# Attention + MLP + mixer kernel: the key sums enter the scores as a float32r matmul, the causal mask is a constant, and layer-1 weights are converted ahead on another timetable

## The chip, the cores and the metric

One core of a Trainium2 chip runs the whole program in one launch. The metric is the device time of that core in microseconds; three runs of the kernel before are shown, and one more execution was profiled.

## What is computed

Attention over 4 batches and 8 heads (576 tokens, head size 64), then two feed-forward layers of 512 x 2048 x 512; the second is preceded by a rank-32 mixing along the tokens. The first layer norms its input.

```python
s_pos = np.maximum(s, 0.0)
cum = np.cumsum(s_pos, axis=-1)
bias = -(cum[:, :, :, None] - cum[:, :, None, :])
scores = np.where(causal, -1000000000.0, scale * q @ k.T + np.minimum(bias, 0.0))
attn = softmax(scores)                      # + 1e-9 in the denominator
x = attn @ v                                # then, per layer:
ch = np.maximum(xn @ w_ch1, 0.0) @ w_ch2    # layer 0: xn = layernorm(x); x = x + ch
xt = x.transpose(0, 2, 1)
h = xt @ U @ V                              # layer 1: u = x + h^T; out = u + ffn(u)
```

Below the diagonal the bias is a difference of key sums, and a softmax row does not change by a constant, so the kernel only needs, for each head, one number per key: the running sum at the key, minus the sum at the end of the row's block of 128 queries. These "key sums" are made once, in `setup`.

## The kernel before, in words

**Tiling.** Every batch is cut into block A (tokens 0 to 255) and block B (256 to 575). Heads are taken in pairs, the two heads of a pair on partitions 0 to 63 and 64 to 127. A pair is worked in ticks: A has one tick (0, 1), B has the ticks (2), (3) and (4), each a block of 128 queries (64 in tick 4). For each tick there is a `score` (matmuls, a DVE reduction that adds the bias and keeps the row's minimum, Exp on ACT, the division), a `trans` (transposes on PE, eviction into `pT`), and after a pair's last tick a `pv` per head. Operands that need more than float32r are split into a high and a low float32r part (`split`: ACT or DVE makes the high part, DVE or POOL the low one). A0 and A1, the A blocks of batches 0 and 1, go in full float32.

**Bias and mask before.** `setup` writes the key sums to a DRAM tensor `cum_dr`. `bias` (L621) reads them back for every head and tick, copied onto all 128 partitions of a tile `t` (L638; L635 for tick 4, 64 partitions a head), and POOL then writes the mask into each such tile (L642). For the first four heads an identity matmul in float32 (L629) and a copy stand in for the load. The DVE reduction in `score` (L696, L678) adds `t` to the scores in PSUM and writes the result over `t`.

**The layers.** 256 steps, 128 a layer: each step is one block of tokens against one slice `m` of 128 hidden units (16 slices, two halves of eight). A step has 12 matmuls in L1053 to L1055 and 12 in L1087 to L1089. The order of steps is in `GROUPS`: layer 0 takes A0 with A1, A2 with A3, then B0 to B3 alone; layer 1 takes (A0, B0) and so on. Weights arrive as float64 in two words; converting one 512 KB half (`f64_to_f32`, then `split`) costs two passes and a split on DVE and ACT each, and the result is written to a DRAM tensor `w_dr`, from which later steps reload it (L506), eight slices being resident (`WSLOTS`). The first eight slices of layer 0 are converted at the start; the others "ahead" of their use by `w_ahead` (L519: one load of 512 KB, L485 or L487, the conversion, and one write of 512 KB, L526).

**What sets the order.** All operations go to a planner (`Plan`) with a priority, a duration per engine it may run on, and buffers; it writes out a fixed order per engine. All transfers are issued by SP in that order. Positions in steps are given by hand: attention of B2 lies in steps 67 to 86 and of B3 in 76 to 100 (`AT`), the conversions of layer 0's second half in 4 to about 12 (`W0`), those of layer 1's 32 halves evenly in 67 to 128 (`W1`). A gated transfer is not issued before the step at its position. Transfers take `nbytes / 400` ns in the planner's own estimate. Until the first step, spare PE time is filled with matmuls on a tile of ones (L1189).

**Buffers.** `t` has 6 tiles, `pA` and `pB` 2 each (`pT` of A and of B), `qk` 2, `wr` (raw weights) 4, `w` 16 halves, PSUM `ps` 6 and `acc` 2.

Of the kernel before, what the change touches and what calls it, by code (L numbers as in the profile page):

```python
# [85 lines left out]
class Plan:  # L86
# [22 lines left out]
    def op(self, prio, alts, reads=(), writes=(), nbytes=0, gate=None, soft=0.0, hold=(), port=False):  # L109
# [3 lines left out]
        o.prio, o.alts, o.nbytes, o.gate = prio, alts, nbytes, gate  # L113
# [29 lines left out]
    def plan(self, prio, price):  # L143
# [37 lines left out]
        while avail:  # L181
# [35 lines left out]
            if o.nbytes:  # L217
                o.end = dma_free = max(dma_free, s + 1100) + o.nbytes / 400.0
# [92 lines left out]
def mha_ffn_mixer_ffn(ctx: ExitStack, tc, qkv_p, qkv_a, qkv_b, s, g, w1, w2, U, V, out):  # L311
# [10 lines left out]
    sb("attn", dict(qk=2, v=1, pA=2, pB=2, t=6, mx=6, sm=4, rc=4))  # L322
# [27 lines left out]
    def load(prio, nbytes, fn, reads, writes, gate=None):  # L350
        P.op(prio, {"sp": (475, fn)}, reads, writes, nbytes, gate)
# [30 lines left out]
    cum_dr = P.fixed(dr_p.tile([B * H, sum(KEYS)], F32, name="cum_dr"))  # L382
# [5 lines left out]
    cums = []  # L388

    def setup():  # L390
        s_sb, cum = (P.buf("pB", [128, 2, 1344]) for _ in range(2))
        cums.append(s_sb)

        def rel(c0, c1):
            return s_sb.tile.rearrange("p a c -> p (a c)")[:R, c0:c1]

        load(PRO, R * S * 4, lambda: nc.sync.dma_start(s_sb[:R, 0, :S], s), [], [s_sb])
# [4 lines left out]
        dve(PRO, S, lambda: nc.vector.tensor_scalar(out=s_sb[:R, 0, :S], in0=s_sb[:R, 0, :S], scalar1=0.0, scalar2=8.0, op0=ALU.max, op1=ALU.mult),  # L402
            [s_sb], [s_sb], 0.521)
        dve(PRO, S, lambda: nc.vector.tensor_tensor_scan(cum[:R, 0, :S], s_sb[:R, 0, :S], s_sb[:R, 0, :S], 0.0, ALU.add, ALU.max),
            [s_sb], [cum], 1.042)

        for i in range(5):
            dve(PRO, KEYS[i], lambda i=i: nc.vector.tensor_scalar(
                out=rel(COL[i], COL[i] + KEYS[i]), in0=cum[:R, 0, :KEYS[i]], scalar1=cum[:R, 0, KEYS[i] - 1:KEYS[i]], scalar2=None, op0=ALU.subtract),
                [cum] + [s_sb] * (i == 0), [s_sb] if i == 0 else [(s_sb, i)], 0.521, 128)  # L410
        for c, (i0, i1) in enumerate(((0, 2), (2, 5))):
            c0, c1 = COL[i0], COL[i1 - 1] + KEYS[i1 - 1]
            load(PRO + 1 + c, R * (c1 - c0) * 4, lambda c0=c0, c1=c1: nc.sync.dma_start(cum_dr[:, c0:c1], rel(c0, c1)),
                 [(s_sb, i) for i in range(i0, i1)], [(cum_dr, i) for i in range(i0, i1)])
# [117 lines left out]
    class Pair:  # L532
# [11 lines left out]
        def load(self, prio, gate):  # L544
# [76 lines left out]
        def bias(self, prio, tick, gate):  # L621
            idx = self.b * H + 2 * self.p
            ts = self.t[tick] = [P.buf("t", [128, S]) for _ in range(1 if tick[0] == 4 else 2)]
            n = sum(KEYS[i] for i in tick)
            c0 = COL[tick[0]]
            for z, t in enumerate(ts):
                if self.full and idx < 4:
                    c = psum()
                    pe(prio, 4 * mm_cost(384), lambda c=c, z=z: nc.tensor.matmul(  # L629
                        c[:, :n], ident[:R, idx + z:idx + z + 1].to_broadcast([R, 128]), cums[0].tile.rearrange("p a c -> p (a c)")[:R, :n],  # L630
                        start=True, stop=True), [ident, (cums[0], 0), (cums[0], 1)], [c])
                    copy(prio, n, lambda c=c, t=t: t[:, :n], lambda c=c: c[:, :n], [c], [t], psum=True)
                elif tick[0] == 4:
                    for y in range(2):
                        load(prio, 256 * n, lambda t=t, y=y: nc.sync.dma_start(  # L635
                            t[64 * y:64 * (y + 1), :n], cum_dr[idx + y:idx + y + 1, c0:c0 + n].to_broadcast([64, n])), [(cum_dr, 4)], [(t, "y%d" % y)], gate)
# [4 lines left out]
                def mask(t, d, cols, base=0):  # L641
                    return lambda: nc.gpsimd.affine_select(out=d(), in_=d(), compare_op=ALU.is_ge, fill=-8e9, base=base, pattern=cols, channel_multiplier=1)  # L642

                if self.blk == "A":
                    d = lambda t=t: t[:, :512].rearrange("p (a c) -> p a c", c=256)[:, :, :128]
                    P.op(prio, {"pool": (360, mask(t, d, [[0, 2], [-1, 128]]))}, [t], [t])
                elif tick[0] < 4:
# [592 lines left out]
```

## Time and profile before

| | |
|---|---|
| median of 3 runs | 1127.78 us (1126.51 to 1134.36) |
| span of the profiled execution | 1120.7 us |
| PE (matmul) busy | 1076.8 us, 96% |
| PE weight load busy | 1020.9 us, 91% |
| DVE / ACT / POOL busy | 603.9 / 490.3 / 176.1 us |
| data moved | 233.38 MB, mean 208 GB/s |

The median of the runs is 7.1 us above the profiled span. "PE" is the matmul, "PEld" the loading of its stationary operand, which overlaps with it; a matmul's end is modelled, so matmuls that follow each other closely overlap in the rows. The DMA share is the mean busy share of the 16 DMA engines.

### The profile page before, as it was taken

How to read it: one execution, taken by the hardware profiler on the slowest of the kernel's cores; microseconds unless marked ns; L12 is line 12 of the kernel's file. 1: busy time of each engine (PE TensorE's matmuls, PEld its weight loads, DVE VectorE, ACT ScalarE, POOL GpSimd, SP SyncE). 2: the span in 40 equal slices, each digit the busy share in tenths (PEclk: the TensorE clock that was granted, in tenths of full speed). 3: DMA queues.
4: the chain of work that ended last, by engine and by line, in shares of the span. 5: the costliest groups of instructions: out<-in, count | busy, mean ns of one | idle time of the engine just before them, and what ended most of it. 6: DMA issues, size and time to landing. Idle time of an engine off the chain costs nothing.

```text
span 1120.7 us, 21017 instructions
## 1 busy us (share of the span) xinstructions
PE 1076.8 (96%) x7830; PEld 1020.9 (91%) x7830; DVE 603.9 (54%) x1442; ACT 490.3 (44%) x1189; POOL 176.1 (16%) x378
## 2 busy tenths in 40 slices
PE   8898899999999989899899999999999999999998
PEld 5587888899999988888799999999999999999998
DVE  6888886865785766777766655421332241233121
ACT  6888765654665645656556433211211121121110
POOL 2225334321331212322311000000000000000000
PEclk9998999999999999999999999999999999999999
DMA  8999996366934699898388689781126114411710
GB/s 287 335 361 289 354 352 204 96 168 228 269 113 124 218 347 297 263 333 269 130 284 280 211 314 411 276 273 57 47 84 219 48 48 165 136 48 48 241 70 33
DMA packets 89637, 233.38 MB, mean 208 GB/s; under 512 B 12896, under 2 KB 32896, under 8 KB 89536
## 3 DMA queue, kind: packets, MB, share of 16 engines
q1 hardware_dynamic: 89536, 232.04, 62.3%
q8 instruction: 62, 1.02, 0.4%
q14 instruction: 39, 0.32, 0.1%
HBM read 186.67 MB, written 54.76 MB: 215 GB/s over the span
## 4 chain that ended last, share of the span: by engine, by line
PE 68%; DMA 17%; DVE 5%; ACT 5%; issue 2%; SPq 2%; POOL 1%; POOLq 0%; DVEq 0%; ACTq 0%
PE ps L1053 10%; PE ps L1054 9%; PE ps L1055 9%; PE acc L1087 7%; PE acc L1088 7%; PE acc L1089 7%; DMA wr<-w2b 3%; PE ps L788 3%; PE ps L741 3%; PE ps L1089 2%; PE ps L1087 2%; PE ps L1088 2%; DMA w<-w_dr 2%; DMA w_dr<-wr 2%; DMA wr<-w1b 2%
## 5 line engine op out<-in xcount | busy, mean ns | idle before, releaser
L1053 PE MATMUL ps<-xh,w 128*128 128x256 f32 (+1 forms) x1024 | 314.0, 307 | 5.5 <-DVE mx L678 2.1
L1055 PE MATMUL ps<-xl,w 128*128 128x256 f32 (+1 forms) x1024 | 304.2, 297 | 0.0
L1054 PE MATMUL ps<-xh,w 128*128 128x256 f32 (+1 forms) x1024 | 304.2, 297 | 0.0
L1060 DVE SCALAR_TENSOR_TENSOR hl<-ps,hh 128x256 fp32r<-128x256 f32 (+1 forms) x256 | 116.2, 454 | 306.2 <-ACT hh L1059 305.3
L1059 ACT ACTIVATE hh<-ps 128x256 fp32r<-128x256 f32 (+1 forms) x256 | 104.1, 407 | 386.9 <-PE ps L1055 386.2
L1087 PE MATMUL acc<-hh,w 128*128 128x256 f32 (+1 forms) x768 | 231.5, 301 | 2.0 <-DMA w<-w_dr 2.0
L1089 PE MATMUL acc<-hl,w 128*128 128x256 f32 (+1 forms) x768 | 225.0, 293 | 0.7 <-DVE hl L1060 0.6
L1088 PE MATMUL acc<-hh,w 128*128 128x256 f32 (+1 forms) x768 | 224.8, 293 | 0.0
L1053 PEld LDWEIGHTS ps<-xh,w 128*128 128x128 f32 x1024 | 195.6, 191 | 11.4 <-DVE mx L678 2.8
L1054 PEld LDWEIGHTS ps<-xh,w 128*128 128x128 f32 x1024 | 195.6, 191 | 0.7
L1055 PEld LDWEIGHTS ps<-xl,w 128*128 128x128 f32 x1024 | 195.3, 191 | 0.0
L1087 PEld LDWEIGHTS acc<-hh,w 128*128 128x128 f32 x768 | 146.9, 191 | 6.8 <-issue 3.4
L1089 PEld LDWEIGHTS acc<-hl,w 128*128 128x128 f32 x768 | 146.9, 191 | 1.2 <-DVE hl L1060 1.1
L1088 PEld LDWEIGHTS acc<-hh,w 128*128 128x128 f32 x768 | 147.2, 192 | 0.3
L702 ACT ACTIVATE t<-t,mx 128x128 f32<-128x128 f32 (+4 forms) x144 | 83.1, 580 | 35.6 <-DVE mx L696 26.5
L1089 PE MATMUL ps<-hl,w 128*128 128x320 f32 x256 | 79.4, 310 | 0.0
L1087 PE MATMUL ps<-hh,w 128*128 128x320 f32 x256 | 79.4, 310 | 0.0
L1088 PE MATMUL ps<-hh,w 128*128 128x320 f32 x256 | 79.4, 310 | 0.0
L741 PE MATMUL ps<-ident,t 128*128 128x128 f32 x400 | 64.9, 278 | 13.0 <-ACT t L715 4.9
L696 DVE CUSTOM_DVE_ANT_0 t<-ps,t 128x128 f32<-128x128 f32 (+3 forms) x128 | 57.3, 485 | 26.0 <-PE ps L692 13.3
L362 POOL TENSOR_TENSOR xl<-x,xh 128x320 fp32r<-128x320 f32 (+1 forms) x7 | 6.0, 867 | 397.4 <-ACT xh L355 377.0
L642 POOL TENSOR_SCALAR_AFFINE_SELECT t<-t 128x128 f32<-128x128 f32 (+2 forms) x128 | 41.4, 326 | 158.1 <-DMA t<-cum_dr 124.4
(129 smaller groups left out, 1545.8 us busy)
## 6 DMA issues: line engine op xcount, KB each, us to landing
w<-w_dr SPq DMA_DIRECT2D x176, 512.0 KB, 6.5
w_dr<-wr SPq DMA_DIRECT2D x48, 512.0 KB, 6.1
t<-cum_dr SPq DMA_DIRECT2D x60, 192.0 KB, 5.2
wr<-w1a SPq DMA_DIRECT2D x16, 512.0 KB, 6.9
wr<-w2a SPq DMA_DIRECT2D x16, 512.0 KB, 7.1
w_dr<-w SPq DMA_DIRECT2D x16, 512.0 KB, 8.3
t<-cum_dr SPq DMA_DIRECT2D x32, 256.0 KB, 5.2
wr<-w1b SPq DMA_DIRECT2D x16, 512.0 KB, 6.0
```

The lines of the kernel that those rows point to most:

```text
L642: return lambda: nc.gpsimd.affine_select(out=d(), in_=d(), compare_op=ALU.is_ge, fill=-8e9, base=base, pattern=cols, channel_multiplier=1)
L696: dve(prio, K, lambda ps=ps, t=t, mx=mx, o=o, K=K, p0=p0, x=x: nc.vector.tensor_tensor_reduce(out=t[:, o:o + K], in0=ps[:, p0:p0 + K], in1 ...
L702: act(prio, K, lambda t=t, mx=mx, o=o, K=K, x=x, y=nt * z + x: nc.scalar.activation(t[:, o:o + K], t[:, o:o + K], AF.Exp, bias=mx[:, (1 if ...
L741: nc.tensor.transpose(ps[:, 128 * j:128 * (j + 1)], t[:, c:c + 128], ident.tile)
L1053: nc.tensor.matmul(ps[:, :n], w[:, 0, sl], xh[:, k, :n], start=k == 0, stop=False)
L1054: nc.tensor.matmul(ps[:, :n], w[:, 1, sl], xh[:, k, :n], start=False, stop=False)
L1055: nc.tensor.matmul(ps[:, :n], w[:, 0, sl], xl[:, k, :n], start=False, stop=k == KT - 1)
L1059: act(st - 1000, n, lambda: nc.scalar.activation(hh[:, :n], ps[:, :n], AF.Relu), [ps], [hh], 51)
L1060: dve(st - 1000, n, lambda: nc.vector.scalar_tensor_tensor(out=hl[:, :n], in0=ps[:, :n], scalar=0.0, in1=f(hh[:, :n]), op0=ALU.max, op1=AL ...
L1087: nc.tensor.matmul(a, w[:, 0, sl], hh[:, :n], start=new, stop=False)
L1088: nc.tensor.matmul(a, w[:, 1, sl], hh[:, :n], start=False, stop=False)
L1089: nc.tensor.matmul(a, w[:, 0, sl], hl[:, :n], start=False, stop=last and (z == 1 or blk == "B"))
```

## The change

1. **Key sums.** The input `s` is loaded four times, onto four groups of 32 partitions, and the key sums are made on all 128. They are kept in SBUF as `ksum` (float32r): groups 0 and 2 hold the rounded value, groups 1 and 3 what rounding left. A constant `sel` holds four 32 x 32 identities. In `score` one matmul per head and key range, with the head's column of `sel` broadcast as the stationary operand and 64 rows of `ksum`, opens the accumulation of the scores in PSUM; the products of q and k follow into the same bank. Only tick 4 still reads its bias from `cum_dr`, which shrinks to that tick.
2. **Mask.** A constant `causal` [128, 512] is made once; the DVE reduction adds it in place of `t`. POOL's mask per tile is left for tick 4 alone.
3. **pv.** The last key block of B (64 keys) is padded: POOL zeroes 64 rows of `v` after each load, and the matmul runs on 128 rows and not on 64.
4. **Buffers.** The `pA` tiles are gone; A's `pT` and the mixer's V tiles come from `pB`.
5. **Conversions ahead.** The 32 halves of layer 1 are placed at 40 to 105 (the first sixteen) and 105 to 142 (the other sixteen; layer 1 begins at step 128).
6. **Planner.** Its transfer rate is 350 bytes per ns, 260 for the broadcast loads of tick 4; a `score` on PE counts one matmul more.

```diff
-    sb("attn", dict(qk=2, v=1, pA=2, pB=2, t=6, mx=6, sm=4, rc=4))
+    sb("attn", dict(qk=2, v=1, pB=2, t=6, mx=6, sm=4, rc=4))
...
-        load(PRO, R * S * 4, lambda: nc.sync.dma_start(s_sb[:R, 0, :S], s), [], [s_sb])
+        for y in range(4):
+            load(PRO, R * S * 4, lambda y=y: nc.sync.dma_start(s_sb[R * y:R * (y + 1), 0, :S], s), [], [(s_sb, "y%d" % y)])
...
+            act(pr, KEYS[i], lambda c0=c0, c1=c1: nc.scalar.activation(ksum[:, c0:c1], rel(c0, c1), AF.Copy), [(s_sb, i)], [(ksum, i)])
+            for y in (1, 3):
+                dve(pr, KEYS[i], lambda y=y, c0=c0, c1=c1: nc.vector.tensor_tensor(
+                    out=ksum[R * y:R * (y + 1), c0:c1], in0=rel(c0, c1)[R * y:R * (y + 1)], in1=f(ksum[R * y:R * (y + 1), c0:c1]), op=ALU.subtract),
+                    [(s_sb, i), (ksum, i)], [(ksum, i)])
...
-                else:
-                    load(prio, 512 * n, lambda t=t, z=z: nc.sync.dma_start(
-                        t[:, :n], cum_dr[idx + z:idx + z + 1, c0:c0 + n].to_broadcast([128, n])), [(cum_dr, i) for i in tick], [t], gate)
...
-                elif tick[0] < 4:
-                    d = lambda t=t: t[:, 128 * tick[0]:128 * (tick[0] + 1)]
-                    P.op(prio, {"pool": (266, mask(t, d, [[-1, 128]]))}, [t], [t])
...
+                        for z in range(2):
+                            r = slice(64 * z, 64 * (z + 1))
+                            nc.tensor.matmul(pss[z][:, p0:p0 + K], sel[r, idx + z:idx + z + 1].to_broadcast([64, 128]), ksum[r, COL[i]:COL[i] + K], start=True, stop=False)
...
-                            out=t[:, o:o + K], in0=ps[:, p0:p0 + K], in1=t[:, o:o + K], scale=-0.125, scalar=3e38, op0=ALU.add, op1=ALU.min,
+                            out=t[:, o:o + K], in0=ps[:, p0:p0 + K], in1=causal[:, 512 - K:], scale=-0.125, scalar=3e38, op0=ALU.add, op1=ALU.min,
...
-                mms = [(j, 0, 320, 64 + 320 * j, 0) for j in range(3)] + [(3, 128, 320, 64 + 1088, 0), (4, 256, 320, 0, 64)]
+                mms = [(j, 0, 320, 64 + 320 * j) for j in range(3)] + [(3, 128, 320, 64 + 1088), (4, 256, 320, 0)]
...
-            put(W0[0] + W0[1] * (k - 2) / 16 if k < 16 else W1[0] + (W1[1] - W1[0]) * (k - 16) / 32, lambda p, g, n=n, z=z: w_ahead(n, z, g))
+            put(W0[0] + W0[1] * (k - 2) / 16 if k < 16 else (40 + 65 * (k - 16) / 16 if k < 32 else 105 + 37 * (k - 32) / 16), lambda p, g, n=n, z=z: w_ahead(n, z, g))
```

How this stands in the program at three places:

SP's queue while layer 0's first eight slices are reloaded for B1 (steps 88 to 95), from the first half of slice m = 4 (`w_dr_4_108`) on; `t` is a bias tile, `wr` a raw weight half of layer 1, `xs` a raw v, and the write to `w_dr_5_125` is that of a converted half of layer 1. Before:

```order
L506 DMA w_7099<-w_dr_4_108 128x1024
L638 DMA t_7117<-cum_dr 128x512
L526 DMA w_dr_5_125<-wr_6941 128x1024
L487 DMA wr_7130<-w2b 128x1024
L506 DMA w_7150<-w_dr_4_108 128x1024
L506 DMA w_7211<-w_dr_5_109 128x1024
L638 DMA t_7233<-cum_dr 128x512
L570 DMA xs_7237<-qkv_b 128x320
L570 DMA xs_7244<-qkv_b 128x320
L638 DMA t_7255<-cum_dr 128x512
L506 DMA w_7258<-w_dr_5_109 128x1024
```

The same place in the changed program:

```order
L522 DMA w_7107<-w_dr_4_111 128x1024
L580 DMA qk_6957<-qkvB_2_161 64x256
L581 DMA qk_6957<-qkvB_2_161 64x64
L522 DMA w_7127<-w_dr_4_111 128x1024
L522 DMA w_7137<-w_dr_5_112 128x1024
L501 DMA wr_7152<-w1b 128x1024
L522 DMA w_7164<-w_dr_5_112 128x1024
L647 DMA t_7186<-cum_dr 64x576 x2
```

The 128-partition loads of `t` are gone, the one left is tick 4's; against these reloads the attention has moved as well: parts of a pair's q and k (`qk`) come here now.

PE's queue at one B score of tick (2), two heads, 384 keys (`ps` two banks). Before, and then after:

```order
L692 MATMUL ps_6510<-qk_5930 128x384
L692 MATMUL ps_6511<-qk_5930 128x384
L692 MATMUL ps_6510<-qk_5930 128x384
L692 MATMUL ps_6511<-qk_5930 128x384
L692 MATMUL ps_6510<-qk_5930 128x384
L692 MATMUL ps_6511<-qk_5930 128x384
```

```order
L693 MATMUL ps_5676<-ksum,sel 128x384
L693 MATMUL ps_5677<-ksum,sel 128x384
L697 MATMUL ps_5676<-qk_4886 128x384
L697 MATMUL ps_5677<-qk_4886 128x384
L697 MATMUL ps_5676<-qk_4886 128x384
L697 MATMUL ps_5677<-qk_4886 128x384
L697 MATMUL ps_5676<-qk_4886 128x384
L697 MATMUL ps_5677<-qk_4886 128x384
```

A pair of matmuls on 64 rows each is put in front of the three pairs.

SP's queue at the end of the first reload of layer 1's second half (slices m = 12 to 15, used in steps 148 to 151). In the program before every write to these slices stands ahead of the first of the sixteen reloads; in the changed one, the last rows are:

```order
L542 DMA w_dr_14_137<-wr_9640 128x1024
L522 DMA w_9889<-w_dr_11_134 128x1024
L522 DMA w_9905<-w_dr_12_135 128x1024
L542 DMA w_dr_15_138<-wr_9732 128x1024
L522 DMA w_9937<-w_dr_12_135 128x1024
L522 DMA w_9947<-w_dr_13_136 128x1024
L542 DMA w_dr_14_137<-wr_9691 128x1024
L522 DMA w_9985<-w_dr_13_136 128x1024
L522 DMA w_10001<-w_dr_14_137 128x1024
L542 DMA w_dr_15_138<-wr_9814 128x1024
L522 DMA w_10034<-w_dr_14_137 128x1024
L522 DMA w_10059<-w_dr_15_138 128x1024
```

Four writes of converted halves now stand among the reloads, the last of each slice two to four rows ahead of the reload that reads it.

## Rows read from the trace of the kernel before

**Rows 1.** The page: the span, and DMA share in 40 slices.
```profile
span 1120.7 us, 21017 instructions
DMA  8999996366934699898388689781126114411710
```

**Rows 2.** Busy time by stretch (columns in the first line; x is instructions).
```profile
core 0: us, PE busy (x) PEld busy (x) DVE busy (x) ACT busy (x) POOL busy (x), PEclk, DMA share, GB/s
0.00:56.00 56.00, 46.66 (x303) 31.11 (x304) 41.91 (x118) 41.73 (x113) 13.08 (x36) 1.00 0.91 311
56.00:224.00 168.00, 153.51 (x1180) 140.92 (x1180) 133.64 (x360) 121.03 (x335) 60.68 (x122) 0.96 0.84 276
224.00:392.00 168.00, 167.83 (x1296) 159.57 (x1295) 112.67 (x278) 97.08 (x225) 43.74 (x102) 1.00 0.62 187
392.00:560.00 168.00, 153.09 (x998) 139.53 (x997) 119.07 (x273) 94.84 (x212) 43.87 (x95) 0.98 0.84 274
560.00:760.00 200.00, 198.93 (x1393) 193.14 (x1392) 104.77 (x216) 79.36 (x171) 12.13 (x22) 1.00 0.81 288
760.00:1092.00 332.00, 332.00 (x2503) 332.00 (x2502) 86.50 (x188) 53.16 (x129) 2.65 (x3) 1.00 0.30 101
```

**Rows 3.** Transfers issued in 392 to 560 us: count, size each, median us to landing.
```profile
DMA packets 18749, 46.02 MB, mean 274 GB/s; under 512 B 2829, under 2 KB 7437, under 8 KB 18733
...
w_dr<-wr SPq DMA_DIRECT2D x14, 512.0 KB, 5.6
...
t<-cum_dr SPq DMA_DIRECT2D x12, 256.0 KB, 5.0
t<-cum_dr SPq DMA_DIRECT2D x13, 192.0 KB, 4.9
```

**Rows 4.** The chain that ended last, two pieces: start us, us, what.
```profile
407.31 8.52 DMA wr<-w1b
...
424.29 7.02 DMA wr<-w2b
```

**Rows 5.** Groups of instructions by line: PE's transposes, and what ended the idle before.
```profile
L741 PE MATMUL ps<-ident,t 128*128 128x128 f32 x400 | 64.9, 278 | 13.0 <-ACT t L715 4.9 <-POOL t L718 4.4 <-DMA wr<-w2b 2.3
```

**Rows 6.** Transfers issued in 56 to 224 us.
```profile
DMA packets 20154, 46.33 MB, mean 276 GB/s; under 512 B 3036, under 2 KB 8839, under 8 KB 20136
...
t<-cum_dr SPq DMA_DIRECT2D x22, 192.0 KB, 5.9
```

**Rows 7.** Transfers issued in 0 to 56 us.
```profile
DMA packets 6525, 17.41 MB, mean 311 GB/s; under 512 B 1220, under 2 KB 2617, under 8 KB 6519
...
t<-cum_dr SPq DMA_DIRECT2D x12, 192.0 KB, 5.7
```

**Rows 8.** Timeline of the first 14 us: two loads of SP, the first DVE reduction.
```profile
1.20 0.89 SPq L550 DMA_DIRECT2D qk<-qkv_p  x2
...
8.76 0.42 DVE L696 CUSTOM_DVE_ANT_0 t<-ps,t 128x256 f32<-128x256 f32 x1 [2.53 <-POOL t L642]
```

**Rows 9.** Groups of instructions by line: one DVE pass of a weight conversion.
```profile
L474 DVE SCALAR_TENSOR_TENSOR ps<-ps,wr 128x512 uint32<-128x512 uint32 (+1 forms) x67 | 45.5, 682 | 27.9 <-ACT wr L472 26.6 <-ACT ps L468 0.7
```

**Rows 10.** The chain: PE's transposes, scores (384, 512 keys), pv of two heads.
```profile
299.06 0.76 PE ps L741 x7
303.83 0.72 PE ps L692 x6
305.14 0.89 PE ps L692 x6
308.52 3.03 PE ps L788 x20
```

**Rows 11.** The chain at 722 us: one MLP matmul of 320 columns.
```profile
722.68 0.15 PE ps L1053
```

**Rows 12.** Transfers issued in 560 to 760 us: reloads of converted weights.
```profile
w<-w_dr SPq DMA_DIRECT2D x64, 512.0 KB, 8.2
```

**Rows 13.** Groups of instructions by line: the identity matmul of the first heads.
```profile
L629 PE MATMUL ps<-pB,ident 32*128 32x384 f32 x8 | 3.6, 532 | 0.0
```

More of the change, by code (lines that the diff above doesn't have):

```diff
@@ L401, in setup @@
         dve(PRO, 128, lambda: nc.vector.memset(ones.tile, 1.0 / DM), [], [ones], 0.521)
-        dve(PRO, S, lambda: nc.vector.tensor_scalar(out=s_sb[:R, 0, :S], in0=s_sb[:R, 0, :S], scalar1=0.0, scalar2=8.0, op0=ALU.max, op1=ALU.mult),
+        P.op(PRO, {"pool": (600, lambda: nc.gpsimd.memset(causal.tile, 0.0))}, [], [causal])
+        for y in range(4):
+            act(PRO, R, lambda y=y: nc.scalar.activation(sel[R * y:R * (y + 1)], ident[R * y:R * (y + 1), R * y:R * (y + 1)], AF.Copy),
+                [ident], [(sel, "y%d" % y)])
@@ L410, in setup @@
                 [cum] + [s_sb] * (i == 0), [s_sb] if i == 0 else [(s_sb, i)], 0.521, 128)
[L411 to L414, printed above, removed]
+            if i == 4:
+                load(pr, R * S * 4, lambda: nc.sync.dma_start(cum_dr.tile, rel(COL[4], COL[4] + S)[:R]), [(s_sb, 4)], [cum_dr])
+                break
@@ L621, in bias @@
         def bias(self, prio, tick, gate):
+            if tick[0] < 4:
+                return
             idx = self.b * H + 2 * self.p
[L623 to L636, printed above, removed]
-                else:
-                    load(prio, 512 * n, lambda t=t, z=z: nc.sync.dma_start(
-                        t[:, :n], cum_dr[idx + z:idx + z + 1, c0:c0 + n].to_broadcast([128, n])), [(cum_dr, i) for i in tick], [t], gate)
[L641 to L646, printed above, removed]
-                elif tick[0] < 4:
-                    d = lambda t=t: t[:, 128 * tick[0]:128 * (tick[0] + 1)]
-                    P.op(prio, {"pool": (266, mask(t, d, [[-1, 128]]))}, [t], [t])
-                else:
-                    for y in range(2):
-                        d = lambda t=t, y=y: t[64 * y:64 * (y + 1), 512:S]
-                        P.op(prio, {"pool": (230, mask(t, d, [[-1, 64]]))}, [(t, "y%d" % y)], [(t, "y%d" % y)])
@@ new lines, in bias @@
+            t = P.buf("t", [128, S])
+            self.t[tick] = [t]
+            for y in range(2):
+                load(prio, 256 * S, lambda t=t, y=y: nc.sync.dma_start(
+                    t[64 * y:64 * (y + 1)], cum_dr[idx + y:idx + y + 1].to_broadcast([64, S])), [cum_dr], [(t, "y%d" % y)], gate, 260.0)
+                d = lambda y=y: t[64 * y:64 * (y + 1), 512:S]
+                P.op(prio, {"pool": (230, lambda d=d: nc.gpsimd.affine_select(
+                    out=d(), in_=d(), compare_op=ALU.is_ge, fill=-8e9, base=0, pattern=[[-1, 64]], channel_multiplier=1))},
+                    [(t, "y%d" % y)], [(t, "y%d" % y)])
@@ L655, in score @@
         def score(self, prio, tick):
+            if tick[0] < 4:
+                self.t[tick] = [P.buf("t", [128, S]) for _ in range(2)]
             ts = self.t[tick]
+            idx = self.b * H + 2 * self.p
             qk, k0, full = self.qk, self.k0, self.full
@@ L726, in trans @@
                 shape = [128, 2, 384 if self.blk == "A" else 1344]
-                self.pT = [P.buf("p" + self.blk, shape, F32 if self.full else F32R) for _ in range(1 if self.full else 2)]
+                self.pT = [P.buf("pB", shape, F32 if self.full else F32R) for _ in range(1 if self.full else 2)]
             pT = self.pT
@@ L927, in mix_prep_v @@
     def mix_prep_v(prio, gate):
-        hi, lo = (P.buf("pA", [128, S], F32R) for _ in range(2))
+        hi, lo = (P.buf("pB", [128, S], F32R) for _ in range(2))
         n = S // 2
```

58 lines of the change are left out of this document (34 added, 24 removed).

## The prediction

> **What bounds the kernel now.** I read busy time by stretch first, because the kernel has regimes [rows 2]. From 760 us on, PE and its weight load are busy in all of 332.00 us: nothing but less PE work would help there. From 224 to 392 us, attention and MLP run side by side and PE still loses next to nothing (167.83 of 168). The time is lost in three stretches. In 0 to 56 us PE mostly waits and is fed with filler. In 56 to 224 us it is idle for 168 - 153.5 = 14.5 us, in 392 to 560 us for 168 - 153.1 = 14.9 us; in both the granted clock is also below 1 on average (0.96, 0.98), so part of them ran at the lower of its two levels, 1.2 GHz. What tells the bad stretches from the good one is the DMA column: 0.91, 0.84 and 0.84 of the 16 engines, against 0.62 in 224 to 392 us. DVE does not tell 392 to 560 us from the good stretch: 119.1 us busy against 112.7, ACT 94.8 against 97.1. In 56 to 224 us DVE (133.6) and ACT (121.0) are heavier too. The slices of the page show the same: 9s up to 168 us, 4s to 9s after, and nearly all 8s and 9s from 392 to 530 us [rows 1].
>
> Then the chain that ended last. In 392 to 450 us it is a string of transfers; single loads of raw weights take 8.52 and 7.02 us there [rows 4]. The direct releasers of PE's idle time are mostly ACT and POOL, which divide the scores ahead of the transposes (4.9 and 4.4 us), a DMA only for 2.3 us [rows 5]. I read these as late because their inputs were late, and come back to it as a rival.
>
> PE's idle time is the smaller of two measures, since a matmul's modelled end covers the start of a pause. The weight load's idle time is the other: 27.1 us in 56 to 224, 28.5 in 392 to 560, and 8.4 in the good stretch, which is what attention costs PE anyway by its own pattern [rows 2]. Against the good stretch, 392 to 560 us thus has 14.9 - 0.2 = 14.7 us of idle time more by matmuls and 28.5 - 8.4 = 20.1 us more by weight loads; I keep both and go between them. The Trainium skill (Perfetto Trace Analysis, "Identifying the Most-Contended Engine") holds matmul busy time to be a bad measure of headroom and the weight load's busy share a good one; taken at its word, that stretch alone would give back 20.1 us and the sum below would be about 2 us larger. The trace agrees so far that matmuls look nearly full in the good stretch while weight loads do not [rows 2].
>
> **The change, part by part.** (a) *Start, 0 to 56 us.* Twelve bias loads of 192 KB go, 2.4 of 17.4 MB [rows 7], 14% of a DMA share of 0.91: at most 0.14 x 0.91 x 56 = 7 us. Against it, three more loads of `s` are issued ahead of everything, 0.45 us each [rows 8], and the first reduction waits for a longer chain on ACT and DVE (rounding, remainder). Before, it began at 8.76 us after 2.53 us of waiting for POOL's mask [rows 8], which it now need not wait for. I take -2 us; bounds -7 (all of the transfer time) and +3 (the loads and the chain, nothing gained).
>
> (b) *56 to 224 us.* At least 22 bias loads go, 4.3 MB of 46.3 [rows 6], with the 256 KB ones about 12% of the bytes; POOL's masks go too, behind which its other work queued. The conversions of this stretch (`W0`) are untouched. Recoverable above the good stretch's level are 27.1 - 8.4 = 18.7 us of weight-load idle time; but DVE and ACT are at 80% and 72% here and remain so. I take a bit under half, -8 us; bounds -2 and -19.
>
> (c) *392 to 560 us.* This is where the two parts meet. 25 bias loads go (12 of 256 KB, 13 of 192 KB: 5.7 MB), and of 14 conversions about half [rows 3]: in the program order, between the reload of layer 0's second half for step 72 and that for step 104, sixteen raw halves were loaded and now eight are. Seven conversions are 7 x 2 x 0.52 = 7.3 MB. So 13.0 of 46.0 MB go, the share falls from 0.84 to 0.60, just that of the good stretch. DVE is spared 7 x 3 passes of 0.68 us, 14 us [rows 9]. If the stretch then behaves as 224 to 392 us does, 14.7 us (by PE) to 20.1 us (by weight load) come back, with 0.02 x 168 = 3 us of slow clock on top. I take -18; bounds -5 (waits really end on ACT) and -22.
>
> (d) *224 to 392 us.* Seven raw halves are loaded before the reload for step 72 and not one: six conversions more, 12 us of DVE on 112.7 and 6.3 MB more; the bias loads that leave are about as many bytes. DVE then stands at 74%, below the 80% of (b). I take +1; bounds 0 and +6.
>
> (e) *560 to 760 us.* Seventeen conversions after the reload for step 104 and not fifteen, stretched to step 142; POOL is nearly empty and DVE at 52% there. +1; bounds 0 and +4.
>
> (f) *PE's own work.* A 384-key score of three pairs takes 0.72 us, a 512-key one 0.89 [rows 10], 0.24 and 0.30 a pair with the cost of entering and leaving; by columns, at 0.15 us for 320 [rows 11], a pair is 0.18 and 0.24. The 16 B pairs thus pay 16 x (0.42 to 0.54) = 6.7 to 8.6 us, A2 and A3, 8 pairs of 128 and 256 keys, 8 x (0.18 to 0.24) = 1.4 to 1.9 us; A0 and A1 pay in a stretch where PE waits anyway. Against it, pv: two heads take 3.03 us for 20 matmuls [rows 10]; by columns the sixteen larger ones take 2 x 2304 / 320 x 0.15 = 2.16 us, so the four small ones on 64 rows take 0.87 us, far over their columns. On 128 rows I bound one from 0.03 us (its columns) to 0.11 (a transpose of 128 columns, 0.76 / 7 [rows 10]): 0.43 to 0.75 us saved per two heads, 6.9 to 12 us in all sixteen pairs. Net -4 to +4; I take -1, since two of the four bounds that go into it are for the small matmuls, and a transpose is the dearer kind. No row shows a broadcast float32r operand on 64 rows; I take the q-k pair beside it as the nearest.
>
> POOL's 32 fills of `v` sit between a load and its split on a queue that loses 96 masks, and the shared `pB` ties A3's last pairs to B0's first ones, both well ahead of their steps: 0, inside the bounds of (d).
>
> Sum: -2 - 8 - 18 + 1 + 1 - 1 = -27 us on the span of 1120.7, so 1093.7 us; with the 7.1 us that lie between the profiled execution and the median of the runs, **1101 us**.
>
> **The rivals.** *The transfers were hidden after all.* The waits that end on ACT and POOL [rows 5] are then a chain of their own; DVE and ACT keep their length, and the lighter queue lets them start no sooner. Then (b) is -2 and (c) -5: -8 in all, 1120 us. Against it speaks that the good stretch has the same DVE and ACT load and no stall [rows 2].
>
> *The later conversions come too late (slower).* Layer 1's second half is first needed at step 144; a slot for it comes free three steps after its last use, five steps ahead, 5 x 24 x 0.15 = 18 us, less 8.2 us of landing [rows 11, 12]: 10 us of slack. The changed queue has four writes among these sixteen reloads. If SP is held at each until the write has landed and the reload after it as well, that is 4 x (5.6 + 8.2) = 55 us [rows 3, 12], 45 beyond the slack: 1146 us. It decides from about 38 us of stall on; below that it eats the gain. For it: a reload right behind its own write. Against: only slices m = 14 and 15 are so placed, they are used last, and writes before them have several rows of reloads in between.
>
> *The sums do not run as pairs.* A float32 identity matmul of 384 columns took 3.6 us for 8 instructions, 0.45 us each, two per product [rows 13]. Should the broadcast operand force that form, one head after the other, the B scores cost 16 x 2 x 0.9 x (1 + 512 / 384) = 67 us and not 8: about 1160 us, slower too. Against it: the operands are declared like q and k, which run in single passes.
>
> *More than forecast.* With no slow clock and (b) at its bound, the sum is about -45: 1083 us.
>
> **How the numbers follow.** Forecast 0.60 (own range 1088 to 1113), transfers hidden after all 0.20, more than forecast 0.09, conversions too late 0.07, no pairs 0.04. Of the hidden case a quarter still comes out faster by over 1% (below 1116.5), and of the late case a third lands within 1%. Faster 0.60 + 0.09 + 0.05 = 0.74; within 1% 0.15 + 0.02 = 0.17; slower 0.09. One per cent is about what a measurement of this kernel can tell from no change. A range of 1083 to 1124 holds the forecast, most of the larger gain and the hidden case.
>
> **What the profile will show.** Right: DMA share near 0.6 and PE idle below 3 us in the stretch that runs steps 72 to 96; no `t<-cum_dr` but tick 4's; the key-sum matmuls of a pair side by side, costing no more than the q-k ones beside them; the first reloads for step 144 landing before their use. Wrong: PE idle unchanged at a lower DMA share (the hidden case); waits of PE on `w<-w_dr` at steps 144 to 153 (late conversions); key-sum matmuls of over 0.3 us busy time per pair; new pauses of PE in 224 to 392 us, where six conversions more are put.

## The result and the profile after

The changed kernel takes 1088.1 us (median of 4 runs, 1085.86 to 1090.13) against 1127.1 us for the kernel before, measured beside it: a ratio of 0.9656, 95% interval 0.9628 to 0.9684. It is faster by 39 us; forecast were 26.8, from 1127.78 to 1101 us, with a range of 1083 to 1124 that holds the result.

The page of the changed kernel: its span, the DMA share and the data rate in 40 slices, and by which engine the chain that ended last was held.

```profile
span 1088.4 us, 20805 instructions
...
DMA  7998993129735693492368599881154116211710
GB/s 240 352 331 309 357 344 112 60 70 335 250 123 171 223 340 129 149 347 99 131 203 299 190 387 373 296 347 50 49 169 141 49 49 219 91 50 52 258 60 34
...
PE 84%; DMA 5%; ACT 5%; DVE 4%; issue 1%; POOL 0%; SPq 0%; ACTq 0%; POOLq 0%; DVEq 0%
```

The string of 9s up to 168 us and the 8s from 392 us on [rows 1] are broken up. The same line of the chain for the kernel before:

```profile
PE 68%; DMA 17%; DVE 5%; ACT 5%; issue 2%; SPq 2%; POOL 1%; POOLq 0%; DVEq 0%; ACTq 0%
```

Transfers held 17% of the chain and now hold 5%. (By itself this share does not rank the kernels of this case, as two experiments below show.) Busy time by stretch, as in [rows 2] (the last two stretches are cut at 728 us, when layer 1 is well under way):

```profile
core 0: us, PE busy (x) PEld busy (x) DVE busy (x) ACT busy (x) POOL busy (x), PEclk, DMA share, GB/s
0.00:56.00 56.00, 50.95 (x378) 38.19 (x379) 49.15 (x138) 47.10 (x132) 9.45 (x26) 1.00 0.83 296
56.00:224.00 168.00, 160.75 (x1303) 148.69 (x1302) 139.53 (x381) 128.22 (x346) 45.13 (x95) 0.98 0.71 245
224.00:392.00 168.00, 166.53 (x1301) 159.04 (x1300) 124.34 (x302) 102.24 (x234) 37.91 (x89) 1.00 0.62 205
392.00:560.00 168.00, 163.43 (x1141) 153.22 (x1141) 114.68 (x279) 99.24 (x223) 37.20 (x85) 0.99 0.55 194
560.00:728.00 168.00, 168.00 (x1184) 165.65 (x1184) 86.42 (x162) 64.43 (x133) 3.46 (x4) 1.00 0.86 314
728.00:1060.00 332.00, 332.00 (x2504) 332.00 (x2503) 85.84 (x188) 53.37 (x129) 2.71 (x3) 1.00 0.32 105
```

PE's idle time falls from 14.5 to 7.25 us in 56 to 224 us and from 14.9 to 4.6 us in 392 to 560 us. DVE and ACT, whose length the first rival held to be the bound, are *busier* than before in 56 to 224 us (139.5 and 128.2 us against 133.6 and 121.0) with PE stalling less. The transfers issued in 392 to 560 us, as in [rows 3], and the transposes' group, as in [rows 5]:

```profile
DMA packets 12395, 32.59 MB, mean 194 GB/s; under 512 B 2045, under 2 KB 4349, under 8 KB 12377
...
w_dr<-wr SPq DMA_DIRECT2D x7, 512.0 KB, 3.5
...
t<-cum_dr SPq DMA_DIRECT2D x14, 144.0 KB, 3.2
```

```profile
L746 PE MATMUL ps<-ident,t 128*128 128x128 f32 x400 | 64.5, 277 | 6.2 <-POOL t L723 2.0 <-DVE x L810 1.4 <-ACT t L720 1.3
```

Seven conversions where fourteen were, only tick 4's `t`, and 6.2 us of idle before the transposes instead of 13.0. For ACT this fits the reading that its waits were late inputs: it does no less in 392 to 560 us than before (99.2 us against 94.8). POOL does less (37.2 against 43.9), since its masks are gone, so for POOL the rows don't show which it was.

Where the time went, step by step. A step begins with its first matmul of L1053 before and of L1058 after (1024 records each, four a step); the table gives that time in us into the span, and how much later than in the changed kernel each of six other profiled executions got there (the last five are experiments below; rate 400 is the run with all transfers planned at 400). Each column is a single execution. The kernel with pv on 64 rows, whose order is that of the changed one, is 1.4 us later at step 0, before its first such matmul, so 1 to 2 us in the table tell nothing.

| step | after | before | new timetable alone | old timetable | bias loads back | rate 400 | rate 300 |
|---|---|---|---|---|---|---|---|
| 0 | 49.6 | +5.5 | +7.8 | +1.9 | +2.9 | +3.0 | +2.9 |
| 40 | 234.9 | +14.8 | +19.2 | +5.8 | +18.5 | +11.4 | +16.5 |
| 64 | 347.2 | +13.1 | +24.8 | +8.1 | +22.3 | +16.6 | +18.9 |
| 112 | 601.8 | +30.2 | +54.5 | +15.5 | +25.2 | +21.9 | +9.4 |
| 128 | 661.3 | +31.0 | +56.4 | +17.3 | +25.2 | +25.5 | +10.3 |
| 160 | 769.7 | +31.8 | +55.5 | +16.4 | +25.1 | +26.9 | +19.0 |
| end | 1088.4 | +32.3 | +56.0 | +16.4 | +25.4 | +26.9 | +19.4 |

The column of the kernel before is the forecast's sum, measured: 5.5 us up to step 0, 9.3 more up to step 40, -1.7 from there to 64, 17.1 from 64 to 112, and 2.1 in all that follows.

### The profile page after: what moved, and what is told of

Read it like the earlier page. It is cut to its first block, busy times and chain, and to the rows that moved or that the text cites. A ratio compares the mean times of both kernels' runs of the same rounds, so it can differ in the third digit from the quotient of the medians.

```text
span 1088.4 us, 20805 instructions
## 1 busy us (share of the span) xinstructions
PE 1066.7 (98%) x7969; PEld 1021.6 (94%) x7969; DVE 605.4 (56%) x1457; ACT 497.7 (46%) x1201; POOL 135.8 (12%) x301
## 2 busy tenths in 40 slices
DMA packets 76483, 213.24 MB, mean 196 GB/s; under 512 B 11456, under 2 KB 23744, under 8 KB 76384
## 4 chain that ended last, share of the span: by engine, by line
PE 84%; DMA 5%; ACT 5%; DVE 4%; issue 1%; POOL 0%; SPq 0%; ACTq 0%; POOLq 0%; DVEq 0%
PE ps L1058 12%; PE ps L1059 11%; PE ps L1060 11%; PE acc L1092 8%; PE acc L1094 8%; PE acc L1093 8%; PE ps L793 4%; PE ps L746 3%; PE ps L1092 3%; PE ps L1093 3%; PE ps L1094 3%; PE ps L697 2%; ACT t L707 1%; PE ps L693 1%; PE ps L675 1%; DMA w<-w_dr 1%
## 5 line engine op out<-in xcount | busy, mean ns | idle before, releaser
L1058 PE MATMUL ps<-xh,w 128*128 128x256 f32 (+1 forms) x1024 | 313.3, 306 | 3.5 <-DVE mx L680 2.6
L1058 PEld LDWEIGHTS ps<-xh,w 128*128 128x128 f32 x1024 | 195.4, 191 | 8.5 <-DVE mx L680 2.9
L360 DVE TENSOR_TENSOR pB<-ps,pB 128x512 fp32r<-128x512 f32 (+2 forms) x114 | 63.4, 570 | 19.2 <-ACT pB L355 18.6
L355 ACT ACTIVATE pB<-ps 128x512 fp32r<-128x512 f32 (+4 forms) x121 | 59.7, 503 | 25.5 <-PE ps L746 23.0
L701 DVE CUSTOM_DVE_ANT_0 t<-ps,causal 128x128 f32<-128x128 f32 (+3 forms) x128 | 56.9, 487 | 10.6 <-PE ps L697 10.0
```

Of the source, the lines that this page charges most:

```text
L355: "act": ((51 if psum else 94) + 0.8333 * n, lambda: nc.scalar.activation(out(), a(), AF.Copy)),
L360: alts = {"dve": (68 + 1.042 * n, lambda: nc.vector.tensor_tensor(out=out(), in0=a(), in1=b(), op=op))}
L1058: nc.tensor.matmul(ps[:, :n], w[:, 0, sl], xh[:, k, :n], start=k == 0, stop=False)
```

## The experiments

Medians of 4 runs or more; the kernel before took 1125.7 to 1127.8 us beside them. All but two start from the changed kernel.

**The key sums with the old timetable.**

```diff
-            put(... if k < 16 else (40 + 65 * (k - 16) / 16 if k < 32 else 105 + 37 * (k - 32) / 16), ...)
+            put(... if k < 16 else W1[0] + (W1[1] - W1[0]) * (k - 16) / 32, ...)
```

> The changed kernel with the 32 conversions of layer 1 back at steps 67 to 128, all else as changed. Theory (transfers: in the stretch of steps 64 to 112 both the bias loads and the crowded conversions load the DMA engines, and either alone leaves them near full): the stretch loses about half of its gain again, 8 to 12 us, and the kernel takes about 1098 us; steps 0 to 64 take as long as in the changed kernel within 2 us. Rival (the key sums alone free enough of the queue; the timetable is worth nothing): 1086 to 1091 us.

1107.0 us, ratio 0.9811 (0.9769 to 0.9854): the timetable is worth 19 us on top of the key sums, more than was expected. 7.4 of them are lost between steps 64 and 112 (8.1 to 15.5), where the conversions lie. The stretch 392 to 560 us of this kernel:

```profile
392.00:560.00 168.00, 157.62 (x1054) 143.62 (x1053) 123.98 (x290) 105.09 (x232) 31.59 (x80) 0.98 0.69 235
```

Its share is between that of before (0.84) and after (0.55), and so is PE's idle time: 10.4 us, against 14.9 and 4.6. The other 8.1 us are lost up to step 64, where this kernel has loaded none of layer 1's raw halves and the changed one six. There its queue has less to carry, so that part of the 19 us is the new order and not the places of the conversions.

**The timetable without the key sums.** The kernel before, with the changed kernel's positions.

```diff
-            put(... if k < 16 else W1[0] + (W1[1] - W1[0]) * (k - 16) / 32, ...)
+            put(... if k < 16 else (40 + 65 * (k - 16) / 16 if k < 32 else 105 + 37 * (k - 32) / 16), ...)
```

> The kernel before with only the new timetable of the conversions (40 to 105, 105 to 142). Theory (transfers): steps 0 to 40 as before within 2 us, the stretch of steps 64 to 112 shorter by 6 to 10 us, the whole about 1118 us. Rival (the timetable is worth nothing by itself, since the bias loads keep the queue full): 1125 to 1130 us. Rival (later conversions come too late for step 144): slower than before, with PE waiting on w<-w_dr at steps 144 to 153.

1147.1 us, ratio 1.0174 (1.0129 to 1.022): slower by 20 us, on the other side of what was expected. The stretch 392 to 560 us:

```profile
392.00:560.00 168.00, 151.45 (x984) 139.86 (x983) 91.76 (x227) 76.04 (x174) 34.07 (x83) 0.96 0.74 235
```

The share falls from 0.84 to 0.74 and PE idles 16.6 us, more than before. DVE and ACT do less here, 91.8 and 76.0 us against 119.1 and 94.8, and the table shows the price between steps 64 and 112 (24.8 to 54.5). That work which PE waits for has moved to later is likely but not shown. The late-conversion rival is not the cause: from step 112 to 160 the lag hardly moves (54.5 to 55.5). So one term of the forecast, "thirteen MB go, the share falls, the stretch then behaves as the good one", doesn't hold by itself.

**The bias loads put back.** 60 loads of 192 KB and 32 of 256 KB are issued again into `t`; the reduction, which writes `t`, waits for each, but adds the constant `causal` and takes the key sums from PSUM, so the loaded values are not used. `t` is also held from the load on.

```diff
+                for z, t in enumerate(ts):
+                    if not (self.full and idx < 4):
+                        load(prio, 512 * n, lambda t=t, z=z: nc.sync.dma_start(
+                            t[:, :n], cum_dr[idx + z:idx + z + 1, :n].to_broadcast([128, n])), [cum_dr], [t], gate, 260.0)
```

> The changed kernel with the bias loads of ticks below 4 issued again into the score tile (from cum_dr, same sizes, 88 loads), before the reduction overwrites it; nothing reads what they bring, but the reduction waits for their landing. No POOL mask. Theory (what the key sums gave is the transfers taken off the queue): most of that part comes back, start 3 to 5 us, steps 8 to 40 about 8 us, steps 64 to 112 about 5 us: about 1105 us. Rival (what they gave is POOL's masks and the shorter chain to the reduction on POOL): 1088 to 1093 us.

1114.7 us, ratio 0.9887 (0.9853 to 0.9922): 26.6 us of the 39 are lost. The table shows where: 15.6 us between steps 0 and 40 and only 2.9 between 64 and 112. The stretch 56 to 224 us, and the group of the DVE reduction (L705 in this kernel):

```profile
56.00:224.00 168.00, 151.42 (x1196) 138.26 (x1196) 126.78 (x341) 116.44 (x317) 38.37 (x82) 0.97 0.83 279
```

```profile
L705 DVE CUSTOM_DVE_ANT_0 t<-ps,causal 128x128 f32<-128x128 f32 (+3 forms) x128 | 57.4, 485 | 14.5 <-PE ps L701 8.6 <-DMA t<-cum_dr 4.8 <-PE ps L697 0.7
```

The share is back at 0.83 and PE's idle time at 16.6 us, while the reduction itself waits only 4.8 us for these loads. Most of the loss is thus not the wait for the bias. In the same stretch PE waits for reloads of weights (engine, line, what it waited for: us, times, longest):

```profile
PE ps L1062 <- DMA w<-w_dr: 3.3, 2, 2.6
PE acc L1096 <- DMA w<-w_dr: 1.5, 1, 1.5
```

In the changed kernel it waits for none there, so other transfers that land later are part of the loss. Holding `t` longer and an order of its own may be others; the run doesn't separate them.

**Bias loads and masks put back.** The same, with POOL's mask on each of these tiles (the line for B; A's masks two blocks at once).

```diff
+                            dd = lambda t=t: t[:, 128 * tick[0]:128 * (tick[0] + 1)]
+                            P.op(prio, {"pool": (266, ... affine_select(out=dd(), in_=dd(), ..., fill=-8e9, ...))}, [t], [t])
```

> The changed kernel with the 88 bias loads of ticks below 4 issued again and POOL's mask written into each such tile again; the reduction waits for both and overwrites them unread. With the loads alone the kernel takes 1114.7 us against 1088.1. Theory (it is the transfers): the masks add little, 1113 to 1119 us. Rival (POOL's masks, queued behind landings, hold up POOL's other work): 1121 us or more, near the kernel before.

1125.7 us, ratio 0.9973 (0.9954 to 0.9993): the masks cost 11 us more, and with both back almost the whole gain is gone. The forecast had mentioned the masks and given them no price of their own. The extra loss isn't spread: this kernel is 1.5 us behind the one above at step 64 and 10 behind at step 104, though only the attention of B2 and B3 is left there. That they sat in PE's way directly is not shown; an order that fits them worse is as likely. Nor does the chain tell of the loss, for transfers hold 7% of it:

```profile
PE 80%; DMA 7%; DVE 5%; ACT 4%; issue 2%; SPq 1%; POOL 1%; DVEq 0%; POOLq 0%; ACTq 0%
```

**pv on 64 rows again.**

```diff
-                    nc.tensor.matmul(ps[:, o0:o1], self.vt(v0 + j, None), pT[k % 2][:, z, c:c + o1 - o0],
+                    p0 = lo.get(j, 0) if blk == "B" else 0
+                    nc.tensor.matmul(ps[:, o0:o1], self.vt(v0 + j, None)[p0:], pT[k % 2][p0:, z, c:c + o1 - o0],
```

> The changed kernel with pv's last key block of B (float32r) on 64 rows again, the padding still written. Theory (entering and leaving the 64-row form costs PE time, 0.43 to 0.75 us per two heads, and PE is the limit where B's pv lies): 5 to 11 us slower than the changed kernel, 1093 to 1099 us. Rival (that time is hidden in waits anyway): within 2 us of 1088 us.

1095.6 us, ratio 0.9713 (0.9677 to 0.975): 7.5 us slower by the median, 5.0 by the profiled spans. Nothing that the planner reads is changed, and in both traces the transfers and the instructions of DVE, ACT and POOL come in the same order, so this loss is the edit's and not an order's. In the chain, two heads of pv (20 matmuls), in this kernel and then in the changed one (start us, us, what):

```profile
263.16 3.03 PE ps L795 x20
```

```profile
260.78 2.58 PE ps L793 x20
```

0.45 us saved, near the lower of the forecast's bounds (0.43 to 0.75).

**The planner's old rate.** Transfers are planned at 400 bytes per ns, all of them. Work, bytes and positions are those of the changed kernel; the order differs, and with it the engine of some operations that may run on several.

```diff
-    def load(prio, nbytes, fn, reads, writes, gate=None, rate=350.0):
+    def load(prio, nbytes, fn, reads, writes, gate=None, rate=400.0):
...
-                    t[64 * y:64 * (y + 1)], cum_dr[...].to_broadcast([64, S])), [cum_dr], [(t, "y%d" % y)], gate, 260.0)
+                    t[64 * y:64 * (y + 1)], cum_dr[...].to_broadcast([64, S])), [cum_dr], [(t, "y%d" % y)], gate, 400.0)
```

> The changed kernel with the planner's old transfer rate (400 bytes per ns for all loads) and nothing else undone; it only moves instructions. Theory A (the lighter queue gives the gain whatever the order): 1086 to 1093 us. Theory B (the gain rests on an order that fits the real transfer times): 1096 us or more.

1114.8 us, ratio 0.9887 (0.9855 to 0.992): 26.7 us of the 39 are gone with all transfers still off the queue. The stretch 120 to 224 us of this kernel, and of the changed one:

```profile
120.00:224.00 104.00, 97.43 (x797) 91.70 (x796) 78.08 (x224) 69.19 (x194) 25.60 (x58) 0.98 0.56 188
```

```profile
120.00:224.00 104.00, 102.09 (x844) 96.55 (x843) 81.27 (x226) 72.19 (x192) 28.62 (x63) 1.00 0.56 194
```

The same DMA share, 0.56, and 6.6 us of PE idle against 1.9. For these two kernels the chain says what the share doesn't: its line on the page, and a piece of it.

```profile
PE 68%; DMA 18%; DVE 6%; ACT 4%; issue 2%; SPq 1%; POOL 0%; ACTq 0%; DVEq 0%; POOLq 0%
```

```profile
154.52 7.82 DMA qk<-qkvA
162.37 0.64 ACT qk L355
163.03 0.70 DVE qk L360
163.78 0.44 PE ps L697 x4
```

A load of q and k takes 7.82 us, its split follows, and the scores come right behind it: in the fixed order this load stands too close to its use. Transfers hold 18% of the chain, much as before the change (17%).

**Rates with the timetable, on the kernel before.** The kernel before with the changed kernel's positions, as above, and the planner at 350 and at 260 for all broadcast loads.

```diff
-    def load(prio, nbytes, fn, reads, writes, gate=None):
+    def load(prio, nbytes, fn, reads, writes, gate=None, rate=350.0):
...
-                        t[:, :n], cum_dr[...].to_broadcast([128, n])), [(cum_dr, i) for i in tick], [t], gate)
+                        t[:, :n], cum_dr[...].to_broadcast([128, n])), [(cum_dr, i) for i in tick], [t], gate, 260.0)
```

> The kernel before with the new timetable and the planner's new transfer rates (350, and 260 for all bias loads), key sums and masks as before. The timetable alone gave 1147.1 us. Theory A (with the bias loads still there, earlier conversions crowd the attention of B0 and B1 and later ones that of B3): stays slower than the kernel before, 1130 us or more. Theory B (the loss of the timetable alone came from an order planned with a wrong transfer rate): 1122 us or less.

1130.1 us, ratio 1.0021 (0.9997 to 1.0045). The rates turn 1147 into 1130 us, 17 us, and timetable and rates together are then worth nothing without the key sums. (What the rates alone do for the kernel before is not known: with its old timetable its planner finds no order at these rates.)

**The rate itself.** Four kernels, each the changed one with the general rate at another value (tick 4's at 260 as in the change): 345, 325, 300 and 400. And one with a constant of the planner moved by 10 ns: what it charges between a transfer's end and the work that waits for it (the expectation names it wrongly). Against landings of 5 to 8 us that is very little. The edits, of 325 and of the last:

```diff
-    def load(prio, nbytes, fn, reads, writes, gate=None, rate=350.0):
+    def load(prio, nbytes, fn, reads, writes, gate=None, rate=325.0):
...
-        return 950
+        return 960
```

> The changed kernel with a planner's rate of 345 and not 350 bytes per ns: no work is changed, only the order that the planner finds. It measures what a new order by itself is worth. If orders differ little: 1085 to 1091 us. If single pieces of 5 us between two kernels can come from the order alone: 1092 us or more, or 1084 us or less.

> The changed kernel with the planner's general transfer rate back at 400 bytes per ns, tick 4's broadcast loads left at 260: between the changed kernel (350 and 260, 1088 us) and the run with 400 and 400 (1115 us). Theory A, the general rate carries the loss: a queue planned at 400 promises buffers earlier than the transfers land, so nearly all of the 27 us are lost again, 1107 to 1118 us. Theory B, the broadcast loads of tick 4 carry it (32 of them per kernel, planned at 400 they are promised 0.1 us early each, but their reader is a score on PE's path): 1086 to 1095 us. Rival, luck of the order: anywhere from 1088 to 1115, unrelated to either.

> The changed kernel with the planner's general rate at 325 bytes per ns, below what the transfers reach where the queue is full (tick 4 stays at 260). Theory A, what matters is that the planner does not promise a landing too early: a little slower a rate costs next to nothing, 1085 to 1095 us. Rival, 350 fits the real rate and any distance from it costs, or the order found at 350 was luck: 1100 us and more.

> The changed kernel with the planner's general rate at 300 bytes per ns. Theory A (promising late is cheap): 1085 to 1098 us, since buffers are planned to come free later than they do and only their slots are lost. Rival, a misfit costs in both directions: 1105 to 1120 us, as at 400.

> The changed kernel with one constant of the planner moved by 10 ns (what it charges SP for a step from one queue entry to the next, 950 to 960), which alters no work, no buffer and no rate, and still gives another order on PE. It measures how much an order found at nearly the same rates differs by itself. If the 27 us of the rate 400 are a matter of the rate: 1085 to 1096 us. If orders scatter that widely by chance: over 1100 us is as likely as not.

| general rate | 300 | 325 | 345 | 350 | 350, 10 ns moved | 400 | 400, tick 4 too |
|---|---|---|---|---|---|---|---|
| median, us | 1109.9 | 1093.7 | 1093.2 | 1088.1 | 1093.3 | 1116.1 | 1114.8 |
| ratio to before | 0.9858 | 0.9716 | 0.9699 | 0.9656 | 0.9714 | 0.9911 | 0.9887 |
| 95% interval | 0.983 to 0.9887 | 0.9691 to 0.974 | 0.9668 to 0.9729 | 0.9628 to 0.9684 | 0.9689 to 0.9739 | 0.9885 to 0.9937 | 0.9855 to 0.992 |

The general rate carries the loss, not tick 4's (whose loads of 144 KB are promised 0.2 us early at 400, not the 0.1 us of the expectation). The two orders at 400 differ by 1.3 us. From 325 to 350 it is level, but for the 5 us by which the change's own order beats its three neighbours (2.3 to 2.8 by the profiled spans), one of which differs in nothing but the 10 ns: that much is luck of the order. 400 and 300 cost 22 to 28 us against the change and 16 to 23 against its neighbours, several times that scatter. At 300 there is one order only. With it, "promising a landing late is cheap" fell. The chain of the kernel planned at 300, where transfers hold no more than in the changed kernel:

```profile
PE 86%; DVE 6%; DMA 5%; ACT 2%; issue 1%; SPq 0%; POOL 0%; DVEq 0%; ACTq 0%
```

Its waits of PE in 126 to 180 us and in 728 to 800 us tell more:

```profile
PE acc L1092 <- DMA w<-w_dr: 6.9, 3, 4.0
```

```profile
PE acc L1092 <- DMA w<-w_dr: 3.5, 1, 3.5
PE acc L1092 <- ACT hh L1064: 2.2, 2, 1.7
```

PE waits for reloads of converted weights, first around steps 16 to 24 and again at steps 144 to 160, where the table jumps from 10.3 to 19.0. The second is the forecast's late-conversion rival, in small. SP's queue ahead of it (start, us, engine, line, transfer):

```profile
735.62 0.32 SPq L542 DMA_DIRECT2D w_dr<-wr  x1
735.99 0.42 SPq L522 DMA_DIRECT2D w<-w_dr  x1
742.84 2.34 SPq L542 DMA_DIRECT2D w_dr<-wr  x2
745.27 1.22 SPq L522 DMA_DIRECT2D w<-w_dr  x2
748.39 0.32 SPq L542 DMA_DIRECT2D w_dr<-wr  x1
748.81 5.75 SPq L522 DMA_DIRECT2D w<-w_dr  x3
```

Nothing is issued between 736.4 and 742.8 us. SP's longest waits from 690 to 760 us are those of a write for its conversion, up to 6.4 us, and the reloads behind it wait with it:

```profile
SPq L542 <- DVE wr L360: 25.2, 8, 6.4
```

## Why the prediction was right, and where it was not

**The direction and the place** were right. The two stretches with a full queue gave most of the gain, the good stretch lost 1.7 us up to step 64 (forecast +1), and 728 to 1060 us is full as before.

**The sum** was -27 us on the span; the spans differ by 32.3. By terms: (a) -5.5 for -2, near the bound of -7, its source not traced (the run with the loads back is 2.9 us later at step 0, but so is the one planned at 300, which has none); (b) -9.3 for -8; (c) -17.1 for -18; (d) +1.7 for +1; (e) -2.1 for +1, with PE waiting nowhere for the later conversions. So (a) and (e) were mis-sized, by 3.5 and 3 us. In (c) the size held, and its premise did so only in part. The stretch was to behave like the good one, which idles 0.2 us by matmuls and 8.4 by weight loads [rows 2]; in the changed kernel 392 to 560 us still idles 4.6 and 14.8, at a DMA share even lower than the good one's (0.55). So it gave back 10.3 and 13.7 us where 14.7 and 20.1 were counted on, and that 17.1 came out near 18 is partly luck. Steps 64 to 112, before and then after:

```profile
360.30:632.00 271.70, 256.03 (x1692) 236.96 (x1692) 190.81 (x426) 154.53 (x343) 58.45 (x123) 0.99 0.80 262
347.20:601.80 254.60, 249.78 (x1730) 236.13 (x1729) 168.27 (x392) 144.45 (x321) 48.54 (x106) 0.99 0.61 212
```

For the 17.1 us saved over these steps, PE's idle time fell by 10.9 us by matmuls and by 16.3 by weight loads. These rows agree with the Trainium skill (Perfetto Trace Analysis, "Identifying the Most-Contended Engine"), which holds the weight load's busy share to be the better measure.

**(f)** was right in both halves. A score of three pairs on 384 keys took 0.72 us [rows 10]; with the key sums it starts here at 309.37 and the next instruction at 310.27:

```profile
309.37 0.44 PE L693 MATMUL ps<-ksum,sel 64*128 64x384 f32 x2
309.65 0.69 PE L697 MATMUL ps<-qk 64*128 64x384 f32 x6
310.27 0.41 PE L793 MATMUL ps<-pB,v 128*128 128x320 f32 x1
```

0.90 us, that is 0.18 for the pair: the lower bound, the price by columns. With 512 keys it is 1.12 us where it was 0.89 [rows 10], 0.23 for the pair. Sixteen of each make 6.6 us, A2 and A3 1.4 to 1.9 at the forecast's price, pv saves 16 x 0.45 = 7.2: about +1 for -1.

**From span to median**, 7.1 us were added, as for the kernel before. That step failed: the changed kernel's median lies 0.3 us *below* its profiled span. A run's time lies about 1.8 us above its own span (1090.13 against 1088.4 us in the changed kernel). The other 5 us were the scatter of the kernel before: its profiled execution was quicker than any of its runs (1124.46 to 1134.36 us), while the changed kernel's profiled run is the slowest of its four. Of the 13 us between 1101 and 1088.1, this step made 7.4 and the sum 5.3.

**The step that was missing** is the change's sixth edit. The planner's rate was described and given no term; it is worth 27 us in the changed kernel, as much as the bias loads. The size of the sum held because the rate in the change was one that fits: the nine slices of the page with a DMA digit of 9 ran at 331 to 387 GB/s, 352 on average, so a queue planned at 400 is promised to be faster than it is. For the forecast that was luck. With the old rate the same edits give 1114.8 us, nearer to the hidden case's 1120 than to 1101. The argument "a lighter queue behaves as the good stretch" was therefore only half of the mechanism. It needs an order made for real landing times: at 400 the queue is as light and two thirds of the gain are gone.

**Where the parts meet** was put wrongly too. The forecast joined loads and conversions in 392 to 560 us. With the loads back, most is lost between steps 0 and 40 (15.6 of 25.4 us), and the old timetable costs 7.4 us between 64 and 112 and 8.1 before. But every one of these runs has an order of its own, and orders alone lose 8.4 and 13.6 us between steps 0 and 40 in the kernels planned at 400 and 300; so where a part acts is shown less surely than that it does. The parts don't add: the key sums with the rates give 20 us (1107.0), the timetable with the rates none (1130.1), all together 39.

**The rivals.** "Transfers were hidden" falls with the loads put back, at rates that fit: 26.6 us, five times what the order alone was seen to do at such rates. "Late conversions" did not come at a rate of 350: no wait of PE on `w<-w_dr` from 560 us on; at 300 it did, and cost 9 us, not the 45 of its price. "No pairs" falls with 0.18 us. "More than forecast", 1083 us, was nearer to the result than the forecast by 8 us, though not by its mechanism: (b) stayed at 9 of its 19 us, and the granted clock in 56 to 224 us is still 0.98.

**The checks that were named.** Steps 72 to 96 run from 385 to 527 us in the changed kernel; DMA share there is 0.59 (said: near 0.6), PE idle 4.6 us (said: below 3, missed):

```profile
385.00:527.00 142.00, 137.43 (x952) 128.58 (x953) 95.36 (x227) 82.51 (x185) 31.91 (x70) 0.99 0.59 204
```

The largest pause left is 2.6 us, a wait of PE for DVE's minimum (L680) of a tick-4 score.

**What stays open.** Why the masks cost 11 us on top of the loads; how much of the 26.6 us is the queue, how much the longer hold of `t` and how much the order; what the planner's new price of a score does (the change adds 200 ns to it beside the fourth matmul, and no run takes them out); and which orders are good: three good ones lie within 0.5 us of each other and the fourth is 5 us better, for no cause that was found. None of the kernels tried beats the changed one.

## What to carry to other kernels

Where a planner writes a static order, its transfer rate is part of the kernel: start from what the full slices of the profile move (here 352 GB/s on average for a planned 350), try values on both sides, and price a change of it like a change of work. Don't judge the queue by the busy share of the DMA engines alone: at one and the same share (0.56 in 120 to 224 us) PE idled 1.9 or 6.6 us. (That the busy share of 16 engines misleads is also what the Trainium skill says: Perfetto Trace Analysis, "Identifying the Most-Contended Engine"; the moved bytes that it would use instead are the same in these two kernels as well, 213.24 MB.) The share of transfers in the chain that ended last told these two apart, 5% against 18%. It is no measure by itself: the kernel planned at 300 has 5% too and is 22 us slower, the one with loads and masks back has 7% and is 38 us slower. What PE waits for, stretch by stretch, says more. And before a gain of a few us is put down to an edit, move an idle constant and see how far the order alone moves the time; here that is 5 us.

## What was not expected of the hardware

The price of a pause is more than the pause. In the kernel planned at 300, PE waits 1.73 and 3.52 us at 744 and 751 us, and the granted clock of the 10 us from 750 on averages 0.66:

```profile
740.00:750.00 10.00, 6.11 (x47) 5.50 (x45) 6.79 (x11) 4.62 (x9) 0.00 (x0) 1.00 0.59 170
750.00:760.00 10.00, 7.90 (x42) 7.48 (x43) 0.42 (x1) 0.38 (x1) 0.00 (x0) 0.66 0.68 257
760.00:770.00 10.00, 10.00 (x74) 10.00 (x73) 3.28 (x6) 1.69 (x4) 0.00 (x0) 1.00 0.35 109
```

So a part of that stretch ran at 1.2 GHz. PE is idle 6 us in these 20, and the kernel falls back 9 us there (10.3 to 19.0 in the table). The same pattern stands in the kernel planned at 400: its granted clock averages 0.79 in 162 to 170 us, and the chain's matmuls of 256 columns after the pause at 162 us take 0.21 us each (the first one longer) where one at full clock, the last line, takes 0.12:

```profile
164.74 0.45 PE acc L1092
165.19 0.21 PE acc L1093
165.40 0.21 PE acc L1094
...
173.17 0.12 PE acc L1092
```
